# Memory keys of two batches formed transposed, softmax scale moved into the exponentials, opening order redone

## The chip, the cores and the metric

One core of one Trainium2 chip. The metric is the device time of one execution in microseconds (us).

## The reference

Attention with 32 memory slots per head, then a gated feed-forward block:

```python
a = exp(phi - max(phi));  a = a / sum(a over s)        # [B, H, S, 32]
k_m = einsum('bhsm,bhsd->bhmd', a, k)                  # memory keys
v_m = einsum('bhsm,bhsd->bhmd', a, v)                  # memory values
attn = softmax(q @ k_m.T / sqrt(D))                    # over the 32 slots
x = (attn @ v_m) -> [B*S, H*D]
out = (silu(x @ w_gate) * (x @ w_val)) @ w_out
# B=8, H=8, S=576, D=64; x is 4608 x 512, the inner width is 1536
```

## The kernel before

The values are folded into the weights first (U = memory values times weights), so the gates are matmuls of U with the softmax result. Batches 0 and 1 run through an opening of some 28 us while the weights still load; all later batches overlap with matmuls of their predecessors. In the opening, `warm(n)` issues filler matmuls, n units of 128 columns each, that are meant to keep TensorE's clock up. The parts that the change touches:

```python
def k_items(b):
    def denominators():
        p = bank([128, NG], FP32, "p_S")
        kv_denominators(b, p)         # 18 matmuls on the exponentials of phi
        kv_reciprocal(b, p)           # rSs[b] = 1/S
        done(p)
    def sums():
        p = [bank([128, D], FP32, f"p_kv{g}") for g in range(NG)]
        kv_sum(b, p, (0,))            # 72 matmuls of 64x32, keys not transposed
        k_norm(b, p)                  # two VectorE scalings by 1/S
        done(*p)
    return [denominators, sums, lambda: kv_T(b, (0,))]   # two transposes, one copy
# v_direct(b): the values by 36 matmuls, already transposed and not scaled,
#              then four VectorE copies; U is scaled by 1/S at its evacuation.
# scores(b,g): 8 matmuls, two ScalarE Exp (scale = 1/8); z_inv(b,g): sums over
#              the 32 slots by 2 matmuls, two Ln, one Exp(-x); norm(b,g): VectorE product.
    ...
    warm(104)
    ...
    z_inv(1, 1)
    v_direct(0)
    nc.scalar.preload_act_table_set("silu_and_others")
    norm(1, 0)
    norm(1, 1)
    warm(24)
    v_direct(1)
    warm(4)
    run([u_half(0, (0,), 0, 0, "av"), u_half(1, (0,), 0, 0, "av")])   # U for the gates
    warm(6)
    for s in range(4):
        gv_gate(0, s)                                                  # first gates
```

The softmax here doesn't subtract the row's maximum and nothing guards it: scores larger than these inputs give would overflow.

## Time and profile before

| | before |
|---|---|
| time, median (range) | 247.63 us (247.25 to 247.68) |
| busy share of TensorE, VectorE, ScalarE | 96%, 66%, 67% |
| first denominators, first gates in the trace | 9.79 us, 28.02 us |
| busy time of TensorE from 28 to 60 us | 31.93 of 32.00 us |

A busy TensorE is not by itself a TensorE that does useful work: the fillers count too. What matters is when the first gate matmul starts, because from there on TensorE is packed to the end. The lines are shown and read in the prediction. In them PE is TensorE's matmuls, PEld its weight loads, DVE is VectorE, ACT ScalarE and POOL GpSimd; L and a number is a line of the kernel. `p_kv`, `p_vT` and `p_mT` are sums of keys or values, `t_kT` their transposed copies, `t_E` the exponentials, `t_lz` the logarithms of their sums, `t_A` the softmax result, `p_u` and `t_U` the sums and the scaled copy of U, `p_g` gates.

### The profile page before, as it was taken

How to read it: one execution, taken by the hardware profiler on the slowest of the kernel's cores; microseconds unless marked ns; L12 is line 12 of the kernel's file. 1: busy time of each engine (PE TensorE's matmuls, PEld its weight loads, DVE VectorE, ACT ScalarE, POOL GpSimd, SP SyncE). 2: the span in 40 equal slices, each digit the busy share in tenths (PEclk: the TensorE clock that was granted, in tenths of full speed). 3: DMA queues.
4: the chain of work that ended last, by engine and by line, in shares of the span. 5: the costliest groups of instructions: out<-in, count | busy, mean ns of one | idle time of the engine just before them, and what ended most of it. 6: DMA issues, size and time to landing. Idle time of an engine off the chain costs nothing.

```text
span 245.9 us, 6627 instructions
## 1 busy us (share of the span) xinstructions
PE 235.0 (96%) x2587; PEld 142.2 (58%) x2614; DVE 162.9 (66%) x364; ACT 164.0 (67%) x350; POOL 47.5 (19%) x77
## 2 busy tenths in 40 slices
PE   7989999999999999999999999999999999999993
PEld 2545567774544756477646655476546655567543
DVE  4136799993338688479837888479746886587420
ACT  2747889884086568957895677866995668676201
POOL 8432532000230004053105400070005000000000
PEclk9999999999999999999999999999999999999999
DMA  6999999996999975996994599289316311310143
GB/s 210 205 206 204 201 208 207 255 251 89 194 180 252 253 95 82 218 315 94 189 258 128 90 209 249 67 157 169 79 44 124 64 43 45 85 43 4 44 126 85
DMA packets 42447, 37.00 MB, mean 150 GB/s; under 512 B 15920, under 2 KB 37168, under 8 KB 42416
## 3 DMA queue, kind: packets, MB, share of 16 engines
q0 software_dynamic: 21424, 22.42, 52.4%
q1 hardware_dynamic: 20240, 13.37, 23.4%
q10 hardware_dynamic: 752, 0.79, 0.9%
q8 instruction: 20, 0.33, 0.5%
q14 instruction: 11, 0.09, 0.1%
HBM read 42.47 MB, written 9.44 MB: 211 GB/s over the span
## 4 chain that ended last, share of the span: by engine, by line
PE 92%; DVE 3%; issue 2%; ACT 1%; DMA 1%
PE p_oo L538 36%; PE p_g L478 20%; PE p_v L478 19%; PE p_u L435 5%; PE p_warm L649 4%; PE p_kv L233 2%; PE p_g L384 1%; DVE t_qT L374 1%; PE p_g L405 1%; DMA out_dram<-t_o 1%; PE p_v L405 1%; DVE t_kT L349 1%; DVE t_A L415 1%; PE p_T L293 1%; ACT t_E L394 0%
## 5 line engine op out<-in xcount | busy, mean ns | idle before, releaser
L538 PE MATMUL p_oo<-WO,t_h 128*128 128x512 bf16 x393 | 101.8, 379 | 3.0 <-issue 2.9
L494 ACT ACTIVATE t_sg<-p_g 128x288 bf16<-128x288 f32 x192 | 76.3, 413 | 34.0 <-PE p_g L478 27.1
L501 DVE TENSOR_TENSOR t_h<-t_sg,p_v 128x288 bf16<-128x288 bf16 x192 | 82.3, 450 | 17.4 <-PE p_v L478 12.9
L478 PEld LDWEIGHTS <-t_U 128*128 128x128 bf16 x768 | 73.9, 98 | 31.7 <-issue 2.7
L478 PE MATMUL p_g<-t_A,t_U 128*128 128x288 bf16 x384 | 77.5, 286 | 0.5
L478 PE MATMUL p_v<-t_A,t_U 128*128 128x288 bf16 x384 | 76.9, 286 | 0.0
L538 PEld LDWEIGHTS <-t_h 128*128 128x128 bf16 x420 | 39.5, 98 | 41.0 <-issue 5.9
L550 DVE COPY t_o<-p_oo 128x512 f32<-128x512 f32 x27 | 18.6, 690 | 31.4 <-PE p_oo L538 31.3
L459 DVE CAST t_U<-p_u 128x512 bf16<-128x512 f32 x42 | 26.7, 683 | 6.8 <-PE p_u L435 6.8
L455 ACT CAST t_U<-p_u 128x512 bf16<-128x512 f32 x30 | 15.8, 592 | 7.7 <-PE p_u L435 7.7
L548 ACT COPY t_o<-p_oo 128x512 f32<-128x512 f32 x8 | 4.7, 588 | 20.0 <-PE p_oo L538 19.9
L114 POOL DMA_DIRECT2D t_q<-in_q_dram x6 | 4.8, 802 | 60.4 <-DMA t_qT<-t_q 58.9
L435 PE MATMUL p_u<-W,t_kT 64*32 64x512 bf16 (+1 forms) x416 | 16.0, 365 | 0.3 <-DVE t_kT L349 0.2
L649 PE MATMUL p_warm<-bones 128*128 128x512 bf16 (+2 forms) x46 | 13.5, 424 | 1.7 <-DVE bones L672 1.7
L213 POOL COPY t_mark<-t_A 1x1 bf16<-1x1 bf16 x4 | 0.7, 179 | 58.3 <-DVE t_A L415 58.3
L415 DVE TENSOR_TENSOR t_A<-t_E,t_lz 128x576 bf16<-128x576 bf16 x16 | 11.4, 750 | 0.0
L394 ACT ACTIVATE t_E<-p_g 128x288 bf16<-128x288 f32 x16 | 6.6, 412 | 7.0 <-PE p_v L384 6.5
L410 ACT ACTIVATE t_lz<-t_lz 128x576 f32<-128x576 f32 x16 | 10.9, 683 | 0.5
L636 ACT ACT_TABLE_LOAD x7 | 9.0, 1283 | 1.4 <-PEq L838 1.3
L461 DVE TENSOR_SCALAR t_U<-p_u,t_rS 128x512 bf16<-128x512 f32 (+1 forms) x14 | 8.8, 668 | 1.4 <-PE p_u L435 1.4
L435 PEld LDWEIGHTS <-t_kT 64*32 64x32 bf16 x416 | 4.9, 89 | 8.2 <-issue 6.7
L457 ACT ACTIVATE t_U<-p_u,t_rS 128x512 bf16<-128x512 f32 (+1 forms) x14 | 8.1, 628 | 1.6 <-PE p_u L435 1.6
(66 smaller groups left out, 167.9 us busy)
## 6 DMA issues: line engine op xcount, KB each, us to landing
t_kv<-in_k_dram POOLq DMA_DIRECT2D x8, 576.0 KB, 9.1
t_kv<-in_v_dram POOLq DMA_DIRECT2D x8, 576.0 KB, 13.5
out_dram<-t_o SPq DMA_DIRECT2D x23, 192.0 KB, 2.4
t_phi<-in_phi_dram POOLq DMA_DIRECT2D x6, 576.0 KB, 16.0
t_q<-in_q_dram POOLq DMA_DIRECT2D x6, 576.0 KB, 7.4
out_dram<-t_o SPq DMA_DIRECT2D x24, 128.0 KB, 2.4
WO<-in_moe_w_out_dram POOLq DMA_DIRECT2D x3, 512.0 KB, 19.2
out_dram<-t_o SPq DMA_DIRECT2D x23, 64.0 KB, 2.0
```

Of the source, the lines that this page charges most:

```text
L410: nc.scalar.activation(out=lz, in_=lz, func=AF.Exp, scale=-1.0)
L415: nc.vector.tensor_tensor(out=a, in0=es.pop((b, g)), in1=lzs.pop((b, g)), op=ALU.mult)
L435: nc.tensor.matmul(p[g][32 * i:32 * i + 32, o:o + n], lhsT=kTs[b][64 * g:64 * g + 64, 2, 32 * i:32 * i + 32], rhs=w_part(w, c, i, g, halve ...
L455: nc.scalar.copy(out=t, in_=p)
L459: nc.vector.tensor_copy(out=t, in_=p)
L478: nc.tensor.matmul(p[:, 0:HALF], lhsT=Us[b, c, g][:, o // 2, which, 128 * (o % 2):128 * (o % 2 + 1)], rhs=atts[b, g][:, r], start=(g == 0) ...
L494: nc.scalar.activation(out=sg, in_=gate[:, 0:HALF], func=AF.Silu)
L501: nc.vector.tensor_tensor(out=dst, in0=sg, in1=val[:, 0:HALF], op=ALU.mult)
L538: nc.tensor.matmul(mine["p"], lhsT=hts[c, jf][:, 128 * u:128 * (u + 1)], rhs=WO[jf], start=(jf == 0), stop=(jf == NJF - 1),)
L550: nc.vector.tensor_copy(out=t_o, in_=mine["p"])
L636: nc.scalar.preload_act_table_set("natural_log_exp_and_others")
L649: nc.tensor.matmul(p[:, 0:128 * a], lhsT=bones, rhs=x.to_broadcast([128, a, 128]) if a > 1 else bones, start=True, stop=True,)
```

## The change

The intent: form the memory keys of the first two batches directly transposed, as the values already are. This removes a scaling, a transpose and a copy from the road to the scores. The missing division by the denominators S goes into the exponentials as a scale per partition. With the shorter road, the order and the fillers of the opening are set anew.

```diff
+    def direct(b, which):            # the body of the old v_direct, for keys or values
+        ... 36 matmuls into one bank ...
+    rks = {}
-    def k_items(b):
+    def k_items(b, engs):
         def denominators():
             ...
+            nc.vector.tensor_scalar(
+                out=rks[b], in0=rSs[b], scalar1=sm_scale, scalar2=None, op0=ALU.mult
+            )
         def sums():
-            kv_sum(b, p, (0,)); k_norm(b, p)
-        return [denominators, sums, lambda: kv_T(b, (0,))]
+            p = direct(b, 0)
+            ... four copies of 64x128 into kTs[b] ...
+        return [denominators, sums]
...
-            nc.scalar.activation(..., func=AF.Exp, scale=sm_scale)
+            scale = rks[b][:, g:g + 1] if b in rks else sm_scale
+            nc.scalar.activation(..., func=AF.Exp, scale=scale)
...
-        lz = att.tile([128, 2, HALF], FP32, tag="lz", name="t_lz")
+        lz = att.tile([128, 2, HALF], FP32, tag="lz", bufs=3, name="t_lz")
...
-    warm(2)
-    scores(1, 1)
-    z_inv(1, 0)
-    z_inv(1, 1)
-    v_direct(0)
+    warm(3)
+    z_inv(1, 0)
+    scores(1, 1)
+    warm(6)
+    v_direct(0, "vvvv")
+    z_inv(1, 1)
     nc.scalar.preload_act_table_set("silu_and_others")
     norm(1, 0)
     norm(1, 1)
-    warm(24)
-    v_direct(1)
+    warm(16)
+    v_direct(1, "vvvv")
     warm(4)
     run([u_half(0, (0,), 0, 0, "av"), u_half(1, (0,), 0, 0, "av")])
-    warm(6)
```

Earlier fillers change as well (8, 10, 3, 2, 3, 2, 4, 2 units become 8, 4, 2, 2, 6, 3, 2, 3), and the keys of batch 1 move within the order.

## The prediction

> **What bounds the kernel now.** I read the page first (busy shares, the 40 slices), then the busy time by stretch, then the timeline of the opening 30 us, engine by engine, and last GpSimd's waits, because they date the landings of the loads. The page:
>
> ```profile
> PE 235.0 (96%) x2587; PEld 142.2 (58%) x2614; DVE 162.9 (66%) x364; ACT 164.0 (67%) x350; POOL 47.5 (19%) x77
> ...
> DMA  6999999996999975996994599289316311310143
> ```
>
> TensorE works 96% of the span, and the DMA engines are full in the first 8 slices (some 49 us). The change touches only the attention of batches 0 and 1, all before 28 us. The stretch after it, from the view of busy time by stretch (length, then busy time of PE):
>
> ```profile
> 28.00:60.00 32.00, 31.93 (x324) 21.24 (x325) 27.12 (x62) 26.77 (x63) 4.92 (x7) 1.00 1.17 211
> ```
>
> From 28 us on PE is packed: 31.93 of 32.00 us. So what the opening saves is kept one for one, unless a load arrives too late for the earlier start. The question is therefore only: how much earlier does the first gate matmul (28.02 us) start? The timeline of its last 4 us:
>
> ```profile
> 24.74 0.74 POOL L141 DMA_DIRECT2D W<-in_moe_w_val_dram  x1 [2.12 <-DMA t_kv<-in_v_dram]
> 24.76 1.43 DVE L415 TENSOR_TENSOR t_A<-t_E,t_lz 128x576 bf16<-128x576 bf16 x2
> 25.05 0.77 PEld L338 LDWEIGHTS <-t_kv 128*64 128x64 bf16 x36 [0.42 <-issue]
> 25.18 0.76 PE L338 MATMUL p_vT<-t_mphi,t_kv 128*64 128x64 bf16 x36
> 25.36 1.28 ACT L728 ACT_TABLE_LOAD   x1
> ...
> 26.09 0.74 POOL L156 DMA_DIRECT2D WO<-in_moe_w_out_dram  x1 [0.60 <-DMA W<-in_moe_w_gate_dram]
> 26.19 0.39 PEld L435 LDWEIGHTS <-t_kT 64*32 64x32 bf16 x9 [0.23 <-DVE t_A L415]
> 26.22 0.96 DVE L349 CAST t_kT<-p_vT 64x64 bf16<-64x64 f32 x4
> 26.32 0.45 PE L435 MATMUL p_u<-W,t_kT 64*32 64x256 bf16 x9
> 26.68 0.47 ACT L457 ACTIVATE t_U<-p_u,t_rS 128x256 bf16<-128x256 f32 x1
> ...
> 27.22 0.89 DVE L461 TENSOR_SCALAR t_U<-p_u,t_rS 128x256 bf16<-128x256 f32 x2
> ```
>
> Two kinds of wait meet here. Loads: GpSimd issues them in order and each issue waits for the one eight before it, so its waits date landings. Values of batch 1 land by 24.74, the first gate weights by 26.09. In the same way: keys of batch 1 by 15.29, queries of batch 1 by 17.73 and 19.06, values of batch 0 by 21.89. Engines: VectorE finishes the second softmax product only at 26.19, so the value copies of batch 1 begin at 26.22 although their matmuls ended at 25.94, and its share of U (the weights times the values) starts at 27.22. ScalarE's table load ends at 26.64, so its share of U starts at 26.68. The gates wait for both shares.
>
> **What the Trainium skill says.** "ScalarE: Activation LUTs", section "What ACT_TABLE_LOAD costs": a per-partition scale operand adds about 93 ns, and a table load takes about 1283 ns. The trace agrees: the load is 1.28 us, and with a scale operand (second line) the same shape is 684 - 592 = 92 ns longer:
>
> ```profile
> L455 ACT CAST t_U<-p_u 128x512 bf16<-128x512 f32 x30 | 15.8, 592 | 7.7 <-PE p_u L435 7.7
> ...
> L457 ACT ACTIVATE t_U<-p_u,t_rS 128x512 bf16<-128x512 f32 x10 | 6.3, 684 | 1.1 <-PE p_u L435 1.1
> ```
>
> "VectorE: DVE Perf Modes", section on the TRN2 errata: a PSUM source costs 120 cycles plus one per element at 0.96 GHz, 192 ns for 64 columns; the trace has 222, so I keep the measured base. "DMA: Bandwidth & Descriptors", section "Issuing engines are not separate DMA queues": all loads share 16 engines. The full DMA row agrees, so nothing the compute does brings a queued load forward. "TensorE: Matmul & The Clock Gate", Part 1: the clock halves after an idle window of about 3.4 us. No gap here is that long, and the granted clock reads 1.00.
>
> **The change, part by part.** The costs that it replaces and reuses:
>
> ```profile
> L269 DVE TENSOR_SCALAR t_bk<-p_kv,t_rS 128x128 bf16<-128x128 f32 x4 | 1.2, 346 | 2.6 <-PE p_kv L233 2.6
> ...
> L349 DVE CAST t_kT<-p_vT 64x64 bf16<-64x64 f32 x8 | 1.8, 222 | 1.7 <-PE p_vT L338 1.5
> ...
> L295 DVE COPY t_kT<-p_T 128x256 bf16<-128x256 bf16 x2 | 0.6, 291 | 0.6 <-PE p_T L293 0.6
> ```
>
> *Keys.* Removed per batch: 72 matmuls (0.64 us in batch 0), two scalings (0.61 us as a pair), two transposes (0.28 us), a copy (0.29 us). Added: 36 matmuls, 0.76 us like the values' 36, and four copies of 64x128. Doubling the columns of the value copy adds 64/0.96 = 67 ns, so about 0.29 us each and, with their pitch of 0.24 + 0.07, 1.2 us for four (an estimate); plus one 128x2 multiply, under 0.17 us (the reciprocal's time) and beside PE. Batch 0: before, the chain took from 10.30 to the end of the copy, 12.35. After: 10.38 + 0.76 + 1.2 = about 12.35. The transposed keys themselves gain nothing in time; they only free PE of a wait on VectorE.
>
> *Scaled exponentials.* Eight activations, 92 ns longer each, 0.7 us of ScalarE in all.
>
> *Order.* Fewer fillers before the queries let q evacuations start at about 13.0 instead of 13.52. Scores (0,0) then start near 13.6 instead of 14.04. From there I walked the order by the measured durations. Keys of batch 1 are ready near 18.0 (19.23 before), scores (1,0) exponentiated from 19.45 (20.41), scores (1,1) from 22.05 (21.99, now behind z of (1,0)). z_inv (1,1) now follows v_direct(0), which cannot start before 21.89: 0.76 us to 22.65, second exponential ends near 22.95, sums, two logs (0.75), the exponential (0.68), end near 24.7 (25.34 before). The table load then ends at about 26.0 (26.64), the last softmax product at about 25.5 (26.19).
>
> *The end of the opening.* Values of batch 1 land by 24.74: matmuls 24.85 to 25.6 (25.18 to 25.94), because 16 filler units replace 24. Copies start at once, 25.65 to 26.6 (26.22 to 27.18). U of batch 0 still waits for the gate weights at 26.09: matmuls 26.2 to 26.5, no gain. Its evacuations start at 26.55 on ScalarE and 26.6 on VectorE and end at 27.0 to 27.05. With the filler of 6 units (0.50 us) gone from in front of the gates, they start at about 27.15. 28.02 - 27.15 = 0.87 us.
>
> *What the loads take back.* The second value weights of chunk 0 land by 30.36 (GpSimd's issue of phi, eight after); their matmuls ran near 31.1, so only 0.7 to 0.8 us can be gained past that point. The value weights of chunk 1 land by 35.18, used at about 36.0 before: 0.8 us. Expected net gain: 0.75 us, which PE carries to the end. 247.63 - 0.75 = 246.9 us, 0.3%.
>
> **Rivals.**
> 1. *The loads hide everything.* The gate weights land at 26.09, where U starts today. For it: the DMA row and that U's first matmul starts 0.1 us later. Against: after it there are 1.7 us to the gates, of which copies, evacuation and filler that waited on engines are 0.9. If the later weights are also a little later than I read, the gain is 0 to 0.3 us: 247.3 to 247.6.
> 2. *The opening is a chain of engine work.* Then the 0.4 to 1.2 us won in the middle, plus the removed fillers, count in full: 1.5 us or more, 246.1. Against: four landings in a row (19.06, 21.89, 24.74, 26.09) cut the chain.
> 3. *ScalarE becomes the bound.* Eight longer exponentials and the later exponential of (1,1) push the table load past 26.6. Its slack in my walk is 0.5 us. If half a microsecond more is lost, the gain shrinks to about 0.4: 247.2.
> 4. *Cooling of PE by missing fillers.* A half-rate stretch of 3 us would cost some 1.5 us: 249. The longest gap that I expect is 0.7 us, so this is unlikely.
>
> **Range and chances.** The middle is 246.9. Rival 1 gives the upper end, 247.5; rival 2 most of the lower, 246.2. Two per cent is 5 us, while the whole stretch between the phi exponentials and the gates is 18 us and nailed to the loads: faster 1%, slower 1%.
>
> **What would show it.** Right: the first gate matmul near 27.15, U of batch 0 still starting at 26.1 to 26.3 with the gate weights landing at about 26.09, value copies of batch 1 ending near 26.6, table load ending before 26.5, key copies near 0.29 us and exponentials near 0.50 us, and PE packed after 28 us with perhaps 0.1 to 0.3 us of waits on weights before 36 us. Wrong: landings themselves that move, U evacuations that wait for the table load, a first gate matmul earlier than 26.9 or later than 27.6, or a span that does not move by the same amount as the first gate.

## The result, and the profile after

The changed kernel took 246.72 us (median of 4 runs, 246.67 to 246.81), the kernel before beside it 247.66 us (247.25 to 247.80). The ratio is 0.9965, with a 95% interval of 0.9948 to 0.9983. Ratios are the mean time of one kernel's fast runs over that of the other's of the same rounds, so not quite the ratio of the medians. The gain of 0.94 us is small but resolved; the forecast was 0.75.

The page of the changed kernel and, below it, its busy time by stretch (bounds and length, busy times of PE, PEld, DVE, ACT and POOL with the number of instructions, granted clock of TensorE, DMA share, GB/s):

```profile
PE 237.5 (97%) x2535; PEld 142.0 (58%) x2535; DVE 164.0 (67%) x368; ACT 165.0 (67%) x350; POOL 47.6 (19%) x77
...
DMA  6999999996999975993995599289226111310143
```

```profile
28.00:60.00 32.00, 32.00 (x323) 21.12 (x323) 27.13 (x62) 26.11 (x61) 4.70 (x7) 1.00 1.15 211
```

TensorE is again packed after 28 us and the DMA engines are again full until about 49 us. TensorE's larger busy total is no sign of more work: the trace of before lacks some matmul records (393 of the 420 of the output product are there), that of after has all of them. What moved is the opening. Its timeline (start, duration, engine, line, operation; in brackets the idle time before it and what ended it):

```profile
24.26 0.77 PEld L321 LDWEIGHTS <-t_kv 128*64 128x64 bf16 x36 [0.42 <-DMA t_kv<-in_v_dram]
24.48 0.74 POOL L141 DMA_DIRECT2D W<-in_moe_w_val_dram  x1 [2.11 <-DMA t_kv<-in_v_dram]
24.64 1.28 ACT L748 ACT_TABLE_LOAD   x1
24.66 0.76 DVE L434 TENSOR_TENSOR t_A<-t_E,t_lz 128x576 bf16<-128x576 bf16 x1 [0.28 <-ACT t_lz L429]
25.45 0.98 DVE L335 CAST t_kT<-p_mT 64x64 bf16<-64x64 f32 x4
25.74 1.04 PE L454 MATMUL p_u<-W,t_kT 64*32 64x256 bf16 x16 [0.27 <-DVE t_kT L335]
25.89 0.74 POOL L156 DMA_DIRECT2D WO<-in_moe_w_out_dram  x1 [0.66 <-DMA W<-in_moe_w_gate_dram]
...
26.46 0.88 DVE L480 TENSOR_SCALAR t_U<-p_u,t_rS 128x256 bf16<-128x256 f32 x2
26.71 1.33 PE L497 MATMUL p_g<-t_A,t_U 128*128 128x288 bf16 x8
```

The table load ends at 25.92 (26.64 before), the last softmax product at 25.42 (26.19). The value copies of batch 1 start at 25.45 (26.22), VectorE's share of U at 26.46 (27.22). There is no filler between U and the gates. The changed kernel's chain of waits (start, duration, what) puts the end of the first eight gate matmuls at 28.04 us, against 29.16 before: 1.12 us earlier.

```profile
25.74 1.04 PE p_u L454 x16
26.78 1.26 PE p_g L497 x8
28.04 0.34 PE p_u L454 x16
```

This lead is still 1.11 us when the output product starts (54.52 and 55.63). In the key and value sums of batch 2, the 72 matmuls are recorded as 0.91 us where they were 0.80, which leaves 1.00 us, and so it stays to the end (spans 244.9 and 245.9).

The costs of the new pieces, from the groups of the opening by shape:

```profile
L335 DVE CAST t_kT<-p_mT 64x128 bf16<-64x128 f32 x8 | 2.3, 289 | 2.1 <-PE p_mT L321 2.0
L335 DVE CAST t_kT<-p_mT 64x64 bf16<-64x64 f32 x8 | 1.8, 223 | 1.2 <-PE p_mT L321 1.0
L348 DVE TENSOR_SCALAR t_rk<-t_rS 128x2 f32<-128x2 f32 x2 | 0.4, 208 | 0.1
```

Key copies take 289 ns and four of them 1.21 us. The extra multiply takes 208 ns, where the prediction said under 0.17 us; the exponentials take 493 ns, as it said. From the first key matmul to the last key copy of batch 0, the way takes 2.01 us (10.51 to 12.52), where the old way took 2.05 (10.30 to 12.35).

### The profile page after: what moved, and what is told of

It reads as the page before. It is cut to its first block, busy times and chain, and to the rows that moved or that the text cites. A ratio compares the mean times of both kernels' runs of the same rounds, so it can differ in the third digit from the quotient of the medians.

```text
span 244.9 us, 6501 instructions
## 1 busy us (share of the span) xinstructions
PE 237.5 (97%) x2535; PEld 142.0 (58%) x2535; DVE 164.0 (67%) x368; ACT 165.0 (67%) x350; POOL 47.6 (19%) x77
## 4 chain that ended last, share of the span: by engine, by line
PE 93%; DVE 2%; ACT 2%; DMA 1%; issue 1%
PE p_oo L557 38%; PE p_g L497 20%; PE p_v L497 20%; PE p_u L454 6%; PE p_warm L668 4%; PE p_kv L233 2%; PE p_g L402 1%; PE p_g L424 1%; DMA out_dram<-t_o 1%; DVE t_qT L392 1%; PE p_q L379 1%; PE p_v L424 1%; ACT t_lz L427 1%; PE p_mT L321 1%; DVE t_kT L335 1%
## 5 line engine op out<-in xcount | busy, mean ns | idle before, releaser
L557 PE MATMUL p_oo<-WO,t_h 128*128 128x512 bf16 x420 | 108.6, 379 | 0.0
L668 PEld LDWEIGHTS <-bones 128*128 128x128 bf16 x43 | 4.5, 112 | 7.3 <-issue 3.5
```

What stands on the lines that cost most here:

```text
L557: nc.tensor.matmul(mine["p"], lhsT=hts[c, jf][:, 128 * u:128 * (u + 1)], rhs=WO[jf], start=(jf == 0), stop=(jf == NJF - 1),)
L668: nc.tensor.matmul(p[:, 0:128 * a], lhsT=bones, rhs=x.to_broadcast([128, a, 128]) if a > 1 else bones, start=True, stop=True,)
```

## The experiments

The theory: the gain comes from the end of the opening, that is from the order of VectorE's and ScalarE's work and from the removed filler, and it ends where the loads land. The first rival: the keys' new route makes the gain. A second question came up on reading the trace of before. Its chain of waits, from the first denominators to the gates, names no load at all (start, duration, what; eight of its 93 pieces):

```profile
9.79 0.59 PE p_S L247 x18
...
11.14 0.61 DVE t_bk L269 x2
...
23.04 0.71 PE p_vT L338 x36
...
24.76 1.43 DVE t_A L415 x2
...
26.98 0.55 PE p_u L435 x7
27.53 0.45 PE p_warm L649 x2
27.98 0.04 issue
28.02 1.14 PE p_g L478 x8
```

The prediction said that four landings cut this chain. If none does, the time depends on when the chain starts, and that start moves. Over the eleven traces here with 104 units of first filler, the first denominators start anywhere from 9.17 to 10.46 us, because the filler matmuls go from one per 0.43 us to one per 0.22 us at a different moment each time: at 5.07 us in e6, 6.33 in before and 6.75 in the changed kernel, whose denominators start at 9.17, 9.79 and 9.99. The start moves by about half as much as that moment. Every profile below is therefore read with its start beside it.

Two times describe each trace: the start of the first denominators, and the end of the first eight gate matmuls in the chain of waits.

| kernel | median, us | ratio to before (95%) | start | gates end |
|---|---|---|---|---|
| before | 247.63 | 1 | 9.79 | 29.16 |
| changed | 246.72 | 0.9965 (0.9948 to 0.9983) | 9.99 | 28.04 |
| e1 order only | 246.92 | 0.9980 (0.9963 to 0.9997) | 9.52 | 28.21 |
| e2 keys only | 247.97 | 1.0023 (1.0006 to 1.0041) | 10.38 | 29.65 |
| e3 before, no filler at the gates | 247.42 | 1.0000 (0.9982 to 1.0018) | 10.46 | 29.20 |
| e4 changed, filler at the gates | 247.20 | 0.9990 (0.9973 to 1.0007) | 9.82 | 28.69 |
| e5 changed, late loads | 249.00 | 1.0048 (1.0025 to 1.0071) | 9.95 | 29.24 |
| e6 before, late loads | 249.34 | 1.0071 (1.0044 to 1.0099) | 9.17 | 29.91 |
| e7 changed, last product late | 246.92 | 0.9973 (0.9952 to 0.9994) | 10.05 | 28.54 |
| e8 changed, two buffers | 247.04 | 0.9989 (0.9953 to 1.0024) | 10.12 | 28.18 |
| e9 before, short first filler | 246.77 | 0.9967 (0.9942 to 0.9992) | 8.82 | 28.27 |
| e10 changed, short first filler | 246.94 | 0.9977 (0.9953 to 1.0002) | 9.11 | 28.21 |
| e11 as e7, short first filler | 246.79 | 0.9969 (0.9946 to 0.9992) | 8.36 | 28.17 |
| e12 changed again | 246.86 | 0.9970 (0.9948 to 0.9993) | 9.66 | 28.33 |

e1 to e4, e5 to e8 and e9 to e12 each ran on one chip beside the kernel before, whose medians there were 247.54, 247.50 and 247.53. All gave correct results.

**e1, the new order with the old keys.**

```diff
-            p = direct(b, 0)            # and four copies, and the scale per partition
+            kv_sum, k_norm, kv_T        # the old route; exponentials with the constant scale
-    run(k0); warm(8); run(k1[:1]); warm(4)
+    run(k0[:2]); warm(8); run(k0[2:] + k1[:1]); warm(4)
-    run(k1[1:]); warm(3); z_inv(0, 1); run(q1[:2])
+    run(k1[1:2]); warm(3); z_inv(0, 1); run(k1[2:] + q1[:2])
```

> The changed kernel with its new order and fillers, but the keys formed the old way (72 narrow matmuls, two scalings, two transposes, a copy) and the exponentials with the constant scale. Theory (the end of the opening, that is landings, the order of VectorE's work and the filler, makes the gain): within 0.2 us of the changed kernel, 246.5 to 246.9. Rival (the keys' new route makes the gain by taking waits off the middle of the chain): most of the gain is lost, 247.3 to 247.7.

Measured: 246.92 us, just outside the 246.5 to 246.9 expected, next to 246.86 for the changed kernel in e12 (on another chip). The new order alone, with the old keys, has the gain within the resolution of these runs. In its trace the gates' chain begins at the landing of the gate weights.

**e2, the new keys in the old order.** The edit is the reverse of e1: the schedule of before, with `k_items` and the exponentials of after.

> The kernel before with its old order and fillers, but the keys formed transposed and the exponentials scaled by 1/S. Theory: the filler in front of the gates and the filler between the value sums stay, so little is gained: 247.3 to 247.7. Rival: most of the gain is here, 246.7 to 247.0.

Measured: 247.97 us. No gain at all, so the first rival falls. It is even slower than the kernel before by about a quarter per cent, which the theory did not foresee. Its profiled execution started 0.59 us later than that of before and ended its gates 0.49 us later, so the chain between the two is 0.10 us shorter. Whether the unprofiled executions also started late, the runs don't show; why the time is longer stays open.

**e3 and e4, the filler of 6 units in front of the gates**, taken from before and given back to after:

```diff
 before:      run([u_half(0, ...), u_half(1, ...)])
-    warm(6)
 after:       run([u_half(0, ...), u_half(1, ...)])
+    warm(6)
```

> The kernel before without the filler of 6 units in front of the first gates. In its trace VectorE's share of U of batch 0 ends at 27.67 and the gates start at 28.02. Theory: the gates start at 27.7, 0.3 us gained, 247.3 to 247.4. If the filler was hidden behind another wait: 247.6.

> The changed kernel with the filler of 6 units put back in front of the first gates. In its trace the sums of U end at 26.78 and the gates run from 26.71 to 28.04 with a short wait for U inside. Theory: the filler takes 0.5 us, of which that wait hides about 0.1: 0.4 us lost, 247.1. If the filler has nothing to do with it: 246.7.

Measured: e4 took 247.20 us, 0.3 us more than e1 beside it and than e12. In its chain U ends at 27.06 and the gates start at 27.55, where the changed kernel has no gap:

```profile
27.06 0.44 PE p_warm L668 x2
...
27.55 1.14 PE p_g L497 x8
```

Its eight gates take 1.14 us instead of 1.26, since they no longer wait for U, so the filler costs 0.49 - 0.12 = 0.37 us net. e3 was inconclusive in time (ratio 1.000): its profiled execution started 0.67 us later than before's and still ended its gates only 0.04 us later. Its trace does decide the filler's share: from the end of U's sums to the end of the gates it takes 29.20 - 27.94 = 1.26 us, where before takes 29.16 - 27.53 = 1.63, the same 0.37 us less. (The way from its start to the end of U's sums is 0.26 us shorter than before's with the same code: 17.48 against 17.74. The chain of before has a gap of 0.44 us there, at 17.05, that no wait explains.)

**e5 and e6, later loads.** One more load of half a megabyte of float32 (256 KB in the DMA view), read by nobody, in front of the first gate weights:

```diff
     load_v(1)
+    extra = wpool.tile([128, NP, HC], BF16, tag="extra", name="extra")
+    nc.gpsimd.dma_start(out=extra, in_=moe_w_gate[:, 0:HC].rearrange("(i p) f -> p i f", p=128))
```

> The changed kernel with one more load of 512 KB of float32 (the first half chunk of the gate weights again, into a tile that nobody reads) queued in front of the first gate weights, so these and all later loads land about 1.3 us later. Theory (the changed opening hangs on the landings): it loses 1.0 to 1.4 us, 247.7 to 248.1. If engine work alone set its end: no loss, 246.7.

> The kernel before with the same extra load. Theory: it has slack behind the landings (filler, copies behind the softmax product), so it loses only 0.3 to 0.6 us, 247.9 to 248.3, and the gap between the two kernels shrinks from 0.9 us to under 0.4. If loads bound neither: no loss, 247.6; if loads bound both alike: the gap stays 0.9.

Measured: 249.00 and 249.34 us. The gap between the two kernels shrinks to 0.34 us, as the theory said, but both lose more than it said. The profiled execution of e5, its fastest (247.97 us), lost what was expected: gates end 1.20 us later, the span is 1.3 us longer. For e6 the busy time by stretch shows what else happened (columns as above):

```profile
24.00:27.40 3.40, 1.31 (x39) 0.75 (x38) 2.18 (x6) 1.72 (x2) 1.48 (x2) 1.00 1.44 196
...
28.50:29.90 1.40, 1.40 (x16) 0.71 (x22) 0.20 (x1) 1.23 (x4) 0.74 (x1) 0.64 1.41 199
29.90:31.50 1.60, 1.60 (x22) 0.83 (x22) 0.88 (x2) 1.55 (x4) 0.74 (x1) 0.50 1.27 208
```

TensorE waited 1.73 us for the gate weights, until 27.43, and 1.5 us after that its clock fell to a half: a mean of 0.64 over 28.50 to 29.90 puts the fall at 28.9, and the view of 31.50 to 33.00 (0.73) the return at 32.3, some 3.4 us later. From the first gate to the U sums of the second half chunk it took 4.31 us (28.33 to 32.64); e5, whose clock stayed at 1.00 after a wait of 1.76 us, took 2.90 (28.09 to 30.99). That the slower, unprofiled executions of e5 also lost clock is likely: their mean granted clock is 0.991 to 0.993, where the profiled one has 0.999 and e6's profiled one 0.993. It is not shown, since one of e11's fastest executions (246.72 us) also reads 0.992. And it is not all: the two slowest of e6 (250.25 and 250.59 us) read 0.999 and 1.000, and their loss stays open. So this pair shows that late loads delay both kernels, and is too disturbed to give the size.

**e7, the last softmax product behind U.** In the changed kernel's timeline above, the value copies of batch 1 wait on VectorE for this product from 25.14 to 25.45.

```diff
     norm(1, 0)
-    norm(1, 1)
     warm(16)
     ...
     run([u_half(0, ...), u_half(1, ...)])
+    norm(1, 1)
```

> The changed kernel with the last softmax product (batch 1, second group) moved on VectorE from in front of the value copies of batch 1 to behind the first shares of U. In the changed kernel's trace the copies wait for it from 25.14 to 25.45. Theory: copies start 0.3 us earlier, the gates about 0.3 us earlier, 246.4 to 246.5. If the landing of the gate weights (about 25.7) already sets the gates: 246.7.

Measured: 246.92 us, beside 247.04 for e8; the difference is not resolved. In its trace the last values landed late (TensorE took them up at 25.15, not 24.26), so there was no wait for the product to take away.

**e8, two buffers for the logarithms.** `bufs=3` of the tile taken out.

> The changed kernel with two instead of three buffers for the logarithms of the sums. In its trace the third one is first written at 20.92 and the first one's reader ends at 20.06. Theory: no wait is added, 246.7. If the third buffer matters: 0.3 us or more lost.

Measured: 247.04 us with a wide interval. The trace decides: start and gates' end both lie 0.13 to 0.14 us after those of the changed kernel, so the third buffer has no part in the gain of this order.

**e9 to e12, a shorter first filler, and the control.**

```diff
-    warm(104)
+    warm(88)
```

> The kernel before with 88 instead of 104 filler units at its very start: 4 matmuls of 512 columns fewer, 0.86 us at the full clock. Its chain of waits from the first denominators (9.79) to the gates holds no landing. Theory (before is a pure engine chain from the end of this filler, with 0.3 to 0.5 us of room to the landings of the last values and the gate weights): it gains 0.5 to 0.8 us, 246.7 to 247.1. Rival (the landings cut the chain, as the prediction held): 0 to 0.3 us, 247.2 to 247.6.

> The changed kernel with the same shorter first filler. Its value sums already start on the landings of the values (21.7 and 24.3) and U on that of the gate weights (25.7). Theory (the change has used up the room to the landings): it gains 0 to 0.3 us over the repeated changed kernel. Rival (engine work still sets it): 0.6 to 0.8 us.

> The changed kernel with the last softmax product behind the first shares of U and the shorter first filler. Theory: the value copies start right after their matmuls (25.15), the gates about 0.3 us before those of the changed kernel, 0.2 to 0.4 us gained over it. If the landing of the gate weights already sets the gates: nothing gained.

> The changed kernel once more, as the control of the runs beside it. Theory: 0.9 us faster than the kernel before where that one's first denominators start near 9.8; its own first denominators may start anywhere from 9.2 to 10.5 us, as in the ten traces so far, and move its gates by less than they move those of the kernel before.

Measured: e9, the kernel before with nothing changed but four filler matmuls at its very start, took 246.77 us: 0.76 us less than before beside it, and no worse than the changed kernel (246.86, which is 0.67 us less than before in these rounds). Its chain starts 0.97 us earlier and its gates end 0.89 us earlier, although TensorE waits once on the way, 0.71 us for the keys of batch 1, which landed late in this execution (16.25 us). Its timeline:

```profile
24.21 0.72 PEld L338 LDWEIGHTS <-t_kv 128*64 128x64 bf16 x36 [0.47 <-DMA t_kv<-in_v_dram]
25.33 0.96 DVE L349 CAST t_kT<-p_vT 64x64 bf16<-64x64 f32 x4
...
26.57 0.50 PE L649 MATMUL p_warm<-bones 128*128 128x512 bf16 x2
27.12 1.14 PE L478 MATMUL p_g<-t_A,t_U 128*128 128x288 bf16 x8
```

Now the value sums of batch 1 start on the landing of the values here as well, but the chain to the gates still goes through the last softmax product, which ends at 25.30. e10 and e11 gain nothing over e12, although they start 0.55 and 1.30 us earlier. Three lines of e12 show why:

```profile
24.94 0.65 PEld L321 LDWEIGHTS <-t_kv 128*64 128x64 bf16 x36 [1.43 <-DMA t_kv<-in_v_dram]
25.74 0.98 DVE L335 CAST t_kT<-p_mT 64x64 bf16<-64x64 f32 x4 [0.65 <-PE p_mT L321]
27.00 1.32 PE L497 MATMUL p_g<-t_A,t_U 128*128 128x288 bf16 x8
```

TensorE idles 1.43 us for the values, VectorE 0.65 us for TensorE. From the first weight load of these value sums to the end of the gates it is 28.33 - 24.94 = 3.39 us. e7, e10 and e11, which took up the values at 25.15, 24.82 and 24.78, need the same: 28.54, 28.21 and 28.17 are each 3.39 us later. Their starts differ by 1.7 us and leave no mark. From that landing on, these executions take the same time, so the changed opening hangs on it there. In the first trace of the changed kernel the values were there at 24.26, and the engine work was the later of the two by 0.4 us (28.04 - 24.26 = 3.78). This work is ScalarE's: it is busy 4.92 of the 5.00 us from 20.92 to 25.92, where before has 4.05, and the last softmax product waits 0.28 us for its last logarithm. So the changed kernel sits where the two meet. The spread of the times fits this on one chip, 0.23 us in six runs of e12 and 1.97 us in the eleven of before beside it, but not on another, where e8's four span 1.66 us and before's eleven 1.61. Only profiled executions show their start, so what makes the spread is not shown. No version here beats it by a resolved amount.

## Why the prediction was right

**The size and the place.** 246.9 was predicted, 246.72 measured; the gain was expected in the last stretch before the gates and is there. The steps in the middle came 0.2 to 0.5 us later than walked (scores (0,0) at 13.80, keys of batch 1 at 18.54), but the end of the table load (26.0 said, 25.92 measured) and of the last product (25.5, 25.42) came out as walked. The key copies (0.29 said, 0.289 measured) and four of them (1.2, 1.21) did too, as did the sentence that the transposed keys gain nothing in time by themselves; e1 and e2 confirm it. That the middle was met so closely is in part luck: at the gates 1.12 us were gained and not 0.87, the loads took back nothing, and how much before loses depends on its moving start.

**Signs that the prediction had set for being wrong.** Three of them showed. The first gate matmul is recorded at 26.71, earlier than the limit of 26.9 (it then waits for U: counted back from 28.04 by the 1.14 us that the eight took before, it would be 26.90). The landings moved: GpSimd's waits put the last values at 24.48 (24.74 before) and the gate weights at 25.89 (26.09). The span moved by 1.00 us where the first gate moved by 1.31. With this goes a step that did not hold. U was to wait for the gate weights until 26.1 to 26.3, with no gain there; its sums start at 25.74, released by the value copies. In the trace of before, too, their wait ends with a softmax product (26.19).

**The filler in front of the gates.** It was named as one of the two gains. It is worth 0.37 us net in the traces of e3 and e4. The rest of the 1.12 us: from the start of the denominators to the end of the first U sums the chain is 26.78 - 9.99 = 16.79 us after and 27.53 - 9.79 = 17.74 before, 0.95 us shorter, less 0.20 for the later start of that execution. 0.75 + 0.37 = 1.12. These are single executions; e3's 17.48 us for the old code shows that some 0.3 us of the 0.95 can be scatter.

**"Copies start at once, 25.65 to 26.6" was only half right.** In the first trace the values came earlier than assumed and the copies still waited 0.31 us for the softmax product. In e12 they do start right after the sums (25.74).

**"What the loads take back" was mis-sized.** It was put at about 0.1 us; from 28 to 36 us TensorE is busy 8.00 of 8.00 us in the changed kernel, so it is nothing. Landings were dated by GpSimd's next issue, and that runs behind: TensorE takes up the last values 0.22 us before that issue (24.26 and 24.48; 24.94 and 25.18 in e12). That the weights had as much more room is inferred from this.

**ScalarE as the bound** (the third rival) came in part: in the changed kernel's first trace the chain runs on ScalarE from 20.92 to 24.63. It did not cost what was feared: the table load is done at 25.92, and ScalarE's share of U waits for the sums (26.10).

**One argument was wrong.** Against the second rival (the opening is a chain of engine work) the prediction held that "four landings in a row cut the chain". For the kernel before they did not: its chain of waits has no load in it, and e9, which starts it 0.97 us earlier, ends the gates 0.89 us earlier. The landings only lay close behind it. As an estimate: the last values landed at about 24.74 - 0.22 = 24.52, and the copies can follow 0.80 us after that (24.94 to 25.74 in e12), so at about 25.3, where they ran at 26.22. No more than about 0.9 us could be won up to the copies; the filler's 0.37 comes on top. The range was right because it took both bounds into account. It also follows that the new keys were not needed for this gain: the new order alone has it, and so has a first filler four matmuls shorter.

**The cooling of TensorE** was called unlikely for the change itself, and did not happen in it. But the reason given, that no gap is 3.4 us long, was not a safe one: in e6 a wait of 1.73 us was followed by a halved clock.

## What to carry to other kernels

In an opening where engine work races the loads, find out for each wait which of the two comes last, and by how much: that margin is the most that shortening the other can give. Before rewriting an operation on such a chain, move its start by a cheap edit, here four filler matmuls; if that alone gives the gain, the rewrite was not what was missing. And date a landing by the engine that waits for it, not by the queue's next issue.

## What the Trainium skill lacked or had wrong

- "TensorE: Matmul & The Clock Gate", Part 1, puts the fall to half clock after an idle window of about 3.4 us. In e6 the granted clock fell to 0.50 at 28.9 us though TensorE's longest wait was 1.73 us, and it was busy 1.63 of the 3.41 us before the fall (25.48 to 28.89); in e5 a wait of 1.76 us left it at 1.00. A gap shorter than the window is not safe. The page does say that the window runs freely and that the warm-up varies from run to run; here the moment when the fillers double their rate goes with starts of the opening from 9.17 to 10.46 us.
- "VectorE: DVE Perf Modes", the section on the TRN2 errata: an estimate from its formula for a PSUM source is 192 and 258 ns for 64 and 128 columns; 223 and 289 were measured. The slope is right, the base is 31 ns short: 150 cycles in place of 120 fit both.
- None of the pages that were read says how much later the issuing GpSimd sees a landing than an engine that waits for it: 0.22 to 0.25 us for the last values in ten traces. (In e8 both read 24.39, but TensorE's idle time there, 0.42 us, is no longer than where before waits for no load.) Nor how much one landing scatters: TensorE took up the same values, on their landing, between 24.21 and 25.15 us in different executions.
